# A planner that learns a margin for logit products and GpSimd's hold on VectorE

## The chip, the cores and the metric

The kernel runs on one core of one Trainium2 chip. A core has five engines that run side by side, each with its own queue of instructions: TensorE (PE, matrix products; PEld is its loading of weights), VectorE (DVE), ScalarE (ACT), GpSimd (POOL) and SyncE (SP, which here issues DMAs). They wait for one another by semaphores. The metric is the time of one execution on the device in microseconds (us), the median of several runs.

## The reference

Two stages follow each other. Attention over a window of 128 positions with a distance bias, and then a layer of eight experts in which each token goes to the expert with the highest logit:

```python
scores = scale * np.matmul(q, k.transpose(0, 1, 3, 2))        # 8 batches, 8 heads, 576 x 64
mask = (rel >= 0) & (rel < window)
scores = np.where(mask, scores + bias[None], -1000000000.0)
attn = np.exp(scores - max); attn = attn / (sum + 1e-09)
x = (attn @ v), transposed to 4608 tokens of 512
...
xn = x / (np.linalg.norm(x, axis=-1, keepdims=True) + 1e-06)
logits = xn @ en.T / tau
expert_idx = np.argmax(logits, axis=1)
gate_w = softmax(logits)[expert_idx]
out[mask] = gate_w * (np.maximum(x[mask] @ w1[e], 0.0) @ w2[e])   # w1[e] 512 x 1024, w2[e] 1024 x 512
```

## The kernel before

The 4608 tokens are 36 tiles of 128, numbered T. Two batches make nine tiles: four of each batch and one "pair" tile that holds the last 64 positions of both. The first tile of a batch has no mask to apply. Each tile is worked in two halves of four heads, so there are 72 score units, u = 2T and 2T + 1.

For a unit the steps are: `score` (TensorE, products into two PSUM banks, `sc`), `merge` and `max` (VectorE), `exp` (ScalarE, tile `pe`), `flip` (TensorE transposes into `ptp`), `phi` (ScalarE) and `plo` (VectorE), which read `ptp` and make the two halves of the split probabilities `pq`, `mask` (GpSimd selects, tiles `md` and `mp`, or `tails` for a pair), `av` (TensorE, products with the values), `recip` and `norm` (VectorE, into `xf`). `flip` and `av` share two PSUM banks, so a `flip` also waits until the `plo` of an earlier unit has read its bank.

For a tile there are besides: the loads of q, k and v (SyncE), the turns of q and k (`ptq`, `ptk`; TensorE, into banks that they share with the logits `ptl` and the ranks `ptr`), the split of v (`v_hi`, and `v_lo` on GpSimd, tile `vo`), `xhi` (a cast of `xf` into the row buffer `gx`, mostly on VectorE), `xlo` (GpSimd subtracts the cast from `xf`), `xdma` (a transposing DMA from `gx` to `xT`, issued by SyncE), `logit` (TensorE, L786 and L790) and `lcopy` (VectorE, the copy of the logits that frees their bank). There are 13 row buffers.

The tiles form groups of 8, 8, 8, 6, 4 and 2. A group that is complete goes through some 22 small routing steps, most of them on VectorE with 2 to 64 numbers a partition (L854 to L882: inverse norms, the greatest logit, a one-hot mark, ranks, the gate), with one set of rank products on TensorE between them; then GpSimd marks each row (`mark`, L886) and sends it by an indirect DMA (`put`, L890 and L891, called a scatter here) to the place of its expert in memory.

When the third group is through, the expert with the most tokens so far is known; its weights are fetched and split in the rest of attention, and the first 384 of its rows are worked as the "head" (`hid` and `out`, L971 and L995), which fills TensorE's gaps at the end of attention. Then come the eight experts in turn, with their own plan.

The order on every engine comes from a planner. The class `Plan` holds a list of jobs, each with an engine, a planned length in ns, what it follows (`after`, a name or a name with extra ns), the buffers that it makes and uses, and a due time. It runs through planned time, takes for each engine the ready job that can start first (among those within a small slack the one that is due first), and so writes the instructions of all engines in one order. Real times come into it only through the numbers in the code. The engines keep that order on the chip, and wait where a real time is later than planned. In this code the lines that matter are these:

```python
f"xdma{T}", "SP", 1320, lambda T=T: x_dma(T), land=1000, moves=1350, after=[f"xlo{T}"]
f"logit{T}", "PE", 210 + SWITCH, lambda T=T: logits_pe(T), after=[f"xdma{T}", enc_done]
f"route{gi}_{i}", e, ns + (45 if e == "DVE" else 0), of(gi, 1, i), after=dep
f"wlo{i}", "DVE", 750, lambda i=i: part_lo(i), after=[f"whi{i}"]
```

Of the kernel before, what the change touches and what calls it, by code (L numbers as in the profile page):

```python
# [71 lines left out]
class Plan:  # L72
# [5 lines left out]
    def job(self, name, eng, ns, emit, after=(), makes=(), uses=(), due=0.0, fill=False, early=0.0, dma=0, land=None, moves=0):  # L78
        after = [a if isinstance(a, tuple) else (a, 0) for a in after]
        self.jobs[name] = dict(  # L80
            name=name, eng=eng, ns=ns, emit=emit, after=after, makes=list(makes), uses=list(uses), due=due, fill=fill, early=early, dma=dma, land=land, moves=moves
# [19 lines left out]
    def run(self, free):  # L101
        jobs, rings, end = self.jobs, {}, {}
        self.landed, moved = {}, 0.0
        left = {n: sum(1 for a, _ in j["after"]) for n, j in jobs.items()}
# [7 lines left out]
        def start(j):  # L112
# [5 lines left out]
            for ring, _ in j["makes"]:  # L118
# [3 lines left out]
                if k >= self.caps[ring]:  # L122
                    if k - self.caps[ring] >= len(lst):
                        return None
                    for u in self.users[lst[k - self.caps[ring]]]:
                        if u not in end:
                            return None
                        t = max(t, self.seen(u, j["name"], end))
            return t

        while len(end) < len(jobs):
# [20 lines left out]
            end[n] = t + j["ns"]  # L152
            free[j["eng"]] = end[n]
# [16 lines left out]
def kernel(  # L170
# [238 lines left out]
    def attention(actx):  # L409
# [611 lines left out]
        def due(stage, u):  # L1021
            return STEP * u + 1000 * DUE[stage]
# [25 lines left out]
        for T in range(NT):  # L1048
# [3 lines left out]
            for n in "kq":  # L1052
# [28 lines left out]
                f"v_lo{T}", "POOL", 1070, lambda T=T: v_lo(T), after=[f"v_hi{T}"],  # L1081
                makes=[(vt + "o", ("vo", T))], uses=[("ldv", T), ("vh", T)], due=due("v", u0) + 1500,
            )
            for hf in range(2):
# [10 lines left out]
                for j in range(2):  # L1095
# [28 lines left out]
                    f"mask{u}", "POOL", 0 if first else 1260 if pair else 1188, lambda a=a: mask_pool(*a), after=[f"plo{u}"] + (["tails"] if pair else []),  # L1124
# [21 lines left out]
                f"xhi{T}", "DVE" if dv else "ACT", 400 if dv else 535, lambda T=T: x_act(T),  # L1146
# [3 lines left out]
                f"xlo{T}", "POOL", 1113, lambda T=T: x_pool(T), after=[f"xhi{T}"], uses=[("xf", T), ("gx", T)],  # L1150
# [7 lines left out]
                f"xdma{T}", "SP", 1320, lambda T=T: x_dma(T), land=1000, moves=1350, after=[f"xlo{T}"], makes=[("xT", ("xT", T))], uses=[("gx", T)],  # L1158
# [3 lines left out]
                f"logit{T}", "PE", 210 + SWITCH, lambda T=T: logits_pe(T), after=[f"xdma{T}", enc_done], makes=[(RING["lg"], ("lg", T))],  # L1162
# [18 lines left out]
        for gi, G in enumerate(groups):  # L1181
# [6 lines left out]
            for i, (e, ns) in enumerate(kinds[0]):  # L1188
                dep = [(x, 1500) for x in prev] if i == R_RANK and not tail else list(prev)
                if i == R_RANK and gi:  # L1190
                    dep.append(f"total{gi - 1}")
                J(
                    f"route{gi}_{i}", e, ns + (45 if e == "DVE" else 0), of(gi, 1, i), after=dep, due=due("route", u) + 150 * i,
# [3 lines left out]
                if i == R_RANK - 1:  # L1197
                    J(f"total{gi}", "DVE", 0 if tail else 250, of(gi, 4, 0), after=prev, due=due("route", u) + 5000)
# [501 lines left out]
```

## Time and profile before

| what | us |
|---|---|
| median of 3 runs | 639.07 |
| lowest and highest run | 637.87, 644.59 |
| profiled execution | 639.91 |
| its span, from the first to the last instruction | 638.1 |
| TensorE busy | 604.2 |
| VectorE busy | 383.5 |
| ScalarE busy | 333.7 |
| GpSimd busy | 257.6 |

The profile shows one execution. Its span is what its rows can tell of, and the 1.8 us between the span and the execution's time lie around it. A row's busy time of TensorE counts overlapping products once. "Idle before" is the time an engine stood still before an instruction, and the name behind the arrow is what released it. Names in rows are the program's tiles without their numbers, with the line of the kernel.

### The profile page before, as it was taken

How to read it: one execution, taken by the hardware profiler on the slowest of the kernel's cores; microseconds unless marked ns; L12 is line 12 of the kernel's file. 1: busy time of each engine (PE TensorE's matmuls, PEld its weight loads, DVE VectorE, ACT ScalarE, POOL GpSimd, SP SyncE). 2: the span in 40 equal slices, each digit the busy share in tenths (PEclk: the TensorE clock that was granted, in tenths of full speed). 3: DMA queues.
4: the chain of work that ended last, by engine and by line, in shares of the span. 5: the costliest groups of instructions: out<-in, count | busy, mean ns of one | idle time of the engine just before them, and what ended most of it. 6: DMA issues, size and time to landing. Idle time of an engine off the chain costs nothing. (4 is left out here: it accounts for less than half of the span.)

```text
span 638.1 us, 16989 instructions
## 1 busy us (share of the span) xinstructions
PE 604.2 (95%) x6661; PEld 407.1 (64%) x6661; DVE 383.5 (60%) x1027; ACT 333.7 (52%) x780; POOL 257.6 (40%) x455
## 2 busy tenths in 40 slices
PE   7999889989979878999999999999999999999996
PEld 4788767768767756454664674674765854754444
DVE  4999799898899999707663245334442364310260
ACT  5999789878978985216451144333332263210210
POOL 7878579969878869610102101101102012001001
PEclk9999899989999989999999999999999999999999
DMA  9999979999999967589939129309248073001001
GB/s 190 210 163 190 202 159 220 197 186 219 208 185 281 243 117 191 162 280 216 334 93 328 61 20 282 116 3 301 100 81 317 18 204 119 17 17 50 13 17 50
DMA packets 213585, 101.49 MB, mean 159 GB/s; under 512 B 195829, under 2 KB 195829, under 8 KB 213504
## 3 DMA queue, kind: packets, MB, share of 16 engines
q1 hardware_dynamic: 207664, 81.47, 59.2%
q0 software_dynamic: 5840, 18.92, 7.9%
q8 instruction: 53, 0.87, 0.6%
q14 instruction: 28, 0.23, 0.1%
HBM read 61.92 MB, written 19.70 MB: 128 GB/s over the span
## 5 line engine op out<-in xcount | busy, mean ns | idle before, releaser
L1399 PE MATMUL ps<-xT,w1h 128*128 128x272 f16 (+7 forms) x896 | 173.5, 293 | 0.8 <-ACT y_head L1001 0.8
L1399 PE MATMUL ps<-xT,w1l 128*128 128x272 f16 (+7 forms) x448 | 131.5, 293 | 0.0
L402 POOL DMA_INDIRECT out_dram<-y,ids x32 | 34.1, 1067 | 238.2 <-DVE y L1457 153.0
L1407 DVE SCALAR_TENSOR_TENSOR hl<-ps,hh 128x272 f16<-128x272 f32 (+7 forms) x112 | 52.1, 474 | 95.0 <-ACT hh L1409 94.9
L1399 PEld LDWEIGHTS <-w1h 128*128 128x128 f16 x896 | 87.7, 98 | 31.2 <-issue 1.1
L1409 ACT ACTIVATE hh<-ps 128x272 f16<-128x272 f32 (+7 forms) x112 | 46.6, 426 | 110.9 <-PE ps L1399 110.2
L1443 PE MATMUL ps<-w2h,hl 128*128 128x512 f16 (+1 forms) x264 | 98.4, 373 | 1.3 <-DVE hl L1407 1.3
L1443 PE MATMUL ps<-w2h,hh 128*128 128x512 f16 (+1 forms) x264 | 98.4, 373 | 0.0
L1443 PE MATMUL ps<-w2l,hh 128*128 128x512 f16 (+1 forms) x264 | 98.4, 373 | 0.0
L651 ACT ACTIVATE pe<-sc,nm 128x128 f32<-128x128 f32 x288 | 85.5, 387 | 10.0 <-DVE nm L644 7.3
L1443 PEld LDWEIGHTS <-hh 128*128 128x128 f16 x528 | 51.5, 98 | 58.2 <-issue 0.8
L500 ACT ACTIVATE pq<-ptp 128x512 f16<-128x512 f32 x72 | 55.2, 767 | 9.8 <-PE ptp L659 9.1
L627 PE MATMUL sc<-kh,qh 64*64 64x192 f32 (+3 forms) x1280 | 59.8, 296 | 0.0
L659 PE MATMUL ptp<-ident,pe 128*128 128x128 f32 x288 | 47.0, 284 | 12.6 <-ACT pe L651 4.4
L503 DVE SCALAR_TENSOR_TENSOR pq<-ptp,pq 128x512 f16<-128x512 f32 x72 | 53.1, 737 | 8.3 <-ACT pq L500 8.1
L644 DVE TENSOR_REDUCE nm<-sc 128x2 f32<-128x256 f32 x144 | 55.9, 409 | 0.8 <-PE sc L627 0.8
L1399 PEld LDWEIGHTS <-w1l 128*128 128x128 f16 x448 | 43.8, 98 | 14.5
L1374 DVE SCALAR_TENSOR_TENSOR w1l<-ws,w1h 128x1024 f16<-128x1024 f32 x28 | 33.3, 1221 | 32.0 <-ACT w1h L1376 31.9
L627 PEld LDWEIGHTS sc<-kh,qh 64*64 64x64 f32 (+1 forms) x1280 | 46.0, 143 | 9.2 <-issue 3.9
L727 PE MATMUL av<-vh,mp 128*128 128x65 f16 (+1 forms) x512 | 43.9, 198 | 2.8 <-POOL spare L890 1.8
L1443 PEld LDWEIGHTS <-hl 128*128 128x128 f16 x264 | 25.8, 98 | 31.7 <-DVE hl L1407 2.6
L1455 ACT ACTIVATE y<-ps,gs 128x512 f32<-128x512 f32 (+1 forms) x16 | 10.7, 668 | 67.1 <-PE ps L1443 65.7
(231 smaller groups left out, 1199.9 us busy)
## 6 DMA issues: line engine op xcount, KB each, us to landing
ws<-moe_w_dram SPq DMA_DIRECT2D x56, 512.0 KB, 6.6
ldk<-k_dram SPq DMA_DIRECT2D x32, 256.0 KB, 4.9
ldq<-q_dram SPq DMA_DIRECT2D x32, 256.0 KB, 5.0
ldv<-v_dram SPq DMA_DIRECT2D x32, 256.0 KB
stg<-moe_w_dram SPq DMA_DIRECT2D x16, 256.0 KB, 4.8
ldk<-k_dram SPq DMA_DIRECT2D x8, 128.0 KB, 4.1
ldq<-q_dram SPq DMA_DIRECT2D x8, 128.0 KB, 4.1
ldv<-v_dram SPq DMA_DIRECT2D x8, 128.0 KB, 5.2
```

Source lines behind the costliest of these rows:

```text
L402: ins = nc.gpsimd.indirect_dma_start(out[:, :], bass.IndirectOffsetOnAxis(ap=ids, axis=0), y, None, bounds_check=NTOK - 1, oob_is_err=False)
L500: nc.scalar.activation(hi, ps, AF.Copy, scale=scale)
L503: nc.vector.scalar_tensor_tensor(lo, ps, scale, hi, op0=ALU.mult, op1=ALU.subtract)
L627: nc.tensor.matmul(sc[T, hf, j][o, l, c], qT[T]["h"][rows, hp, o], x["h"][rows, hp, c.start + at : c.stop + at], start=False, stop=True, s ...
L644: nc.vector.tensor_reduce(nm_t[T, hf, j], sc[T, hf, j][:, :, 0:P], axis=AX.X, op=ALU.min)
L651: nc.scalar.activation(pr_t[T, hf][:, 2 * l + j, :], ps[:, l, 0:P], AF.Exp, bias=nm[:, l : l + 1], scale=-1.0)
L659: nc.tensor.transpose(pt[:, i, :], pe[:, i, :], ident)
L727: nc.tensor.matmul(o_, a_, b_, start=False, stop=(n == last), skip_group_check=True)
L1399: nc.tensor.matmul(ps[:, :w], a[:, kt, fs], xx[:, b + kt, c0 : c0 + w], start=(n == 0), stop=(n == len(jobs) - 1))
L1407: nc.vector.scalar_tensor_tensor(hl[:, ft, c0 : c0 + w], ps[:, :w], 0.0, hi, op0=ALU.max, op1=ALU.subtract)
L1409: nc.scalar.activation(hi, ps[:, :w], AF.Relu)
L1443: nc.tensor.matmul(ps, x[:, ft, a * P : (a + 1) * P], w[:, ft, c], start=(n == 0), stop=(n == len(jobs) - 1))
```

## The change

A job may now have a `lock`, a list of lengths for which it holds VectorE off, one after the other from its planned start, and a mark `port`, which says that it is a VectorE step that such a hold stops. A step with `port` that would start within a hold is planned so that it ends 30 ns behind it. The locks go to GpSimd's `v_lo`, `mask` and `xlo`; the mark goes to `xhi` on VectorE, to `wlo`, to `total`, to one gate step and to the routing steps on VectorE except reciprocals, reductions and those that read PSUM. `total` is planned with 300 ns instead of 250 and `wlo` with 650 instead of 750. For all tiles but the last three, `xdma` is planned 800 ns later behind `xlo` and `logit` 1500 ns later behind `xdma`. No instruction is new and none is gone.

```diff
@@ in Plan.run, start(j)
+            if j["port"]:
+                for a, b in held[-8:]:
+                    if a <= t + 60 < b:
+                        t = max(t, b + 30 - j["ns"])
             return t
...
             end[n] = t + j["ns"]
+            if j["port"]:
+                for a, b in held[-8:]:
+                    if a <= t + 60 < b:
+                        end[n] = max(end[n], b + 30)
+            a = t
+            for d in j["lock"]:
+                held.append((a, a + d))
+                a += d
             free[j["eng"]] = end[n]
...
-                f"v_lo{T}", "POOL", 1070, lambda T=T: v_lo(T), after=[f"v_hi{T}"],
+                f"v_lo{T}", "POOL", 1070, lock=(1070,), emit=lambda T=T: v_lo(T), after=[f"v_hi{T}"],
...
-                    f"mask{u}", "POOL", 0 if first else 1260 if pair else 1188, lambda a=a: mask_pool(*a), after=[f"plo{u}"] + (["tails"] if pair else []),
+                    f"mask{u}", "POOL", 0 if first else 1260 if pair else 1188, lock=() if first else (480, 420, 600) if pair else (590, 590), emit=lambda a=a: mask_pool(*a), after=[f"plo{u}"] + (["tails"] if pair else []),
...
-                f"xhi{T}", "DVE" if dv else "ACT", 400 if dv else 535, lambda T=T: x_act(T),
+                f"xhi{T}", "DVE" if dv else "ACT", 400 if dv else 535, port=bool(dv), emit=lambda T=T: x_act(T),
...
-                f"xlo{T}", "POOL", 1113, lambda T=T: x_pool(T), after=[f"xhi{T}"], uses=[("xf", T), ("gx", T)],
+                f"xlo{T}", "POOL", 1113, lock=(1113,), emit=lambda T=T: x_pool(T), after=[f"xhi{T}"], uses=[("xf", T), ("gx", T)],
...
-                f"xdma{T}", "SP", 1320, lambda T=T: x_dma(T), land=1000, moves=1350, after=[f"xlo{T}"], makes=[("xT", ("xT", T))], uses=[("gx", T)],
+                f"xdma{T}", "SP", 1320, lambda T=T: x_dma(T), land=1000, moves=1350, after=[(f"xlo{T}", 800 if T < NT - 3 else 0)], makes=[("xT", ("xT", T))], uses=[("gx", T)],
...
-                f"logit{T}", "PE", 210 + SWITCH, lambda T=T: logits_pe(T), after=[f"xdma{T}", enc_done], makes=[(RING["lg"], ("lg", T))],
+                f"logit{T}", "PE", 210 + SWITCH, lambda T=T: logits_pe(T), after=[(f"xdma{T}", 1500 if T < NT - 3 else 0), enc_done], makes=[(RING["lg"], ("lg", T))],
...
-                    f"route{gi}_{i}", e, ns + (45 if e == "DVE" else 0), of(gi, 1, i), after=dep, due=due("route", u) + 150 * i,
+                    f"route{gi}_{i}", e, ns + (45 if e == "DVE" else 0), port=e == "DVE" and i not in (3, 7, 11, 14, kinds[2] - 1 if gi == GP else 0, kinds[2], kinds[2] + 2), emit=of(gi, 1, i), after=dep, due=due("route", u) + 150 * i,
...
-                    J(f"total{gi}", "DVE", 0 if tail else 250, of(gi, 4, 0), after=prev, due=due("route", u) + 5000)
+                    J(f"total{gi}", "DVE", 0 if tail else 300, port=not tail, emit=of(gi, 4, 0), after=prev, due=due("route", u) + 5000)
...
-                J(f"gate{gi}_{i}", e, ns, of(gi, 2, i), after=prev, due=due("route", u) + 150 * (i + 14))
+                J(f"gate{gi}_{i}", e, ns, port=i == 3, emit=of(gi, 2, i), after=prev, due=due("route", u) + 150 * (i + 14))
...
-            J(f"wlo{i}", "DVE", 750, lambda i=i: part_lo(i), after=[f"whi{i}"], uses=[("stg", i)], due=d + 5500, fill=True)
+            J(f"wlo{i}", "DVE", 650, port=True, emit=lambda i=i: part_lo(i), after=[f"whi{i}"], uses=[("stg", i)], due=d + 5500, fill=True)
```

The order changes on every engine from about the tenth unit to the end of attention; from the experts on it is the same on all of them. Names below are tiles with the tile's and the half's number; the last number is a buffer's. Lines of the changed kernel stand 13 lower than those of before.

VectorE before, where the third group's routing begins (`rc_2`, `rz_2`) and the `plo` of unit 53 writes `pq_26_1`:

```order
L854 TENSOR_SCALAR rc_2_4941<-gn_2_3322 128x8
L743 RECIPROCAL rs_25_1_4943<-av_25_1_4896 128x4
L749 TENSOR_TENSOR xf_25_4849<-av_25_1_4896,rs_25_1_4943 128x256
L765 CAST gx_25_4959<-xf_25_4849 128x512
L857 RECIPROCAL rz_2_4965<-ry_2_4945 128x8
L858 TENSOR_TENSOR rz_2_4965<-rz_2_4965,gn_2_3322 128x8
L859 TENSOR_TENSOR rz_2_4965<-rz_2_4965,ry_2_4945 128x8
L503 SCALAR_TENSOR_TENSOR pq_26_1_4961<-ptp_26_1_4936,pq_26_1_4961 128x512
```

VectorE now, at the same place:

```order
L778 CAST gx_25_4937<-xf_25_4836 128x512
L516 SCALAR_TENSOR_TENSOR pq_26_1_4935<-ptp_26_1_4915,pq_26_1_4935 128x512
L812 COPY gl_2_3617<-ptl_23_4944 128x16
L657 TENSOR_REDUCE nm0_27_1_5001<-sc0_27_1_4925 128x2
L867 TENSOR_SCALAR rc_2_5005<-gn_2_3366 128x8
L657 TENSOR_REDUCE nm1_27_1_5007<-sc1_27_1_4926 128x2
L756 RECIPROCAL rs_26_0_5019<-av_26_0_4953 128x4
L762 TENSOR_TENSOR xf_26_5021<-av_26_0_4953,rs_26_0_5019 128x256
L870 RECIPROCAL rz_2_5032<-ry_2_5014 128x8
L516 SCALAR_TENSOR_TENSOR pq_27_0_5030<-ptp_27_0_5009,pq_27_0_5030 128x512
L871 TENSOR_TENSOR rz_2_5032<-rz_2_5032,gn_2_3366 128x8
```

The `plo` of unit 53 has moved ahead of all routing steps of the group, and the next one ahead of all but two.

TensorE before, at the logit product of tile 16 (`ptl_16`, from `xT_16`), behind the last score product of unit 39 and ahead of the two turns of tile 21; of its eight products and eight weight loads one of each stands here:

```order
L627 MATMUL sc1_19_1_3549<-kh_18_3049,qh_19_3240 64x192
L786 LDWEIGHTS xT_16_3389
L786 MATMUL ptl_16_3576<-enc_169,xT_16_3389 128x16
L511 MATMUL ptk_21_3591<-ident_68,ldk_21_3014 128x128 x4
L511 MATMUL ptq_21_3610<-ident_68,ldq_21_3051 128x128 x4
L659 MATMUL ptp_19_0_3640<-ident_68,pe_19_0_3571 128x128 x4
```

TensorE now, from the same score product on:

```order
L640 MATMUL sc1_19_1_3537<-kh_18_2910,qh_19_3249 64x192
L524 MATMUL ptk_21_3569<-ident_68,ldk_21_2904 128x128 x4
L672 MATMUL ptp_19_0_3579<-ident_68,pe_19_0_3555 128x128 x4
L799 LDWEIGHTS xT_16_3398
L799 MATMUL ptl_16_3588<-enc_169,xT_16_3398 128x16
L724 MATMUL av_18_1_3600<-eone_76,erow_75 128x4
```

The key turn and the flip of unit 38 (`ptp_19_0`) have moved ahead of the logit product.

GpSimd before, from the subtraction ahead of the first scatter on (`xs<-gx` with the tile's number); the memset that stands ahead of every scatter is not shown:

```order
L776 TENSOR_TENSOR gx_10_2310<-xf_10_2212,gx_10_2310 128x512
L891 DMA xs_66<-gx_0_565,di_0_2361 42496x514
L679 AFFINE_SELECT md_11_1_2405<-pq_11_1_2327 128x512
L679 AFFINE_SELECT mp_11_1_2404<-pq_11_1_2327 128x512
L891 DMA xs_66<-gx_1_733,di_0_2361 42496x514
L679 AFFINE_SELECT md_12_0_2469<-pq_12_0_2421 128x512
L679 AFFINE_SELECT mp_12_0_2468<-pq_12_0_2421 128x512
L891 DMA xs_66<-gx_2_879,di_0_2361 42496x514
```

GpSimd now, from the mask of unit 25 (`md_12_1`) to that of unit 28, again without the memsets:

```order
L692 AFFINE_SELECT md_12_1_2541<-pq_12_1_2493 128x512
L692 AFFINE_SELECT mp_12_1_2540<-pq_12_1_2493 128x512
L904 DMA xs_66<-gx_0_565,di_0_2544 42496x514
L904 DMA xs_66<-gx_1_773,di_0_2544 42496x514
L904 DMA xs_66<-gx_2_879,di_0_2544 42496x514
L789 TENSOR_TENSOR gx_11_2495<-xf_11_2353,gx_11_2495 128x512
L904 DMA xs_66<-gx_3_1029,di_0_2544 42496x514
L904 DMA xs_66<-gx_4_1176,di_0_2544 42496x514
L789 TENSOR_TENSOR gx_12_2656<-xf_12_2554,gx_12_2656 128x512
L904 DMA xs_66<-gx_5_1401,di_0_2544 42496x514
L692 AFFINE_SELECT md_14_0_2851<-pq_14_0_2721 128x512
```

The first three scatters stood one by one behind the masks of units 22, 23 and 24, and now stand in a row behind that of unit 25.

## Rows read from the trace of the kernel before

**Rows 1.** The page's first part: busy us, share of the span, instructions.

```profile
PE 604.2 (95%) x6661; PEld 407.1 (64%) x6661; DVE 383.5 (60%) x1027; ACT 333.7 (52%) x780; POOL 257.6 (40%) x455
```

**Rows 2.** Busy us by stretch: length, engines (instructions), granted clock, DMA share, GB/s.

```profile
0.00:36.00 36.00, 31.40 (x444) 23.35 (x445) 26.04 (x84) 28.64 (x76) 29.62 (x83) 1.00 1.10 196
36.00:252.00 216.00, 195.11 (x3737) 157.34 (x3736) 197.28 (x607) 185.22 (x503) 174.68 (x291) 0.98 1.04 197
252.00:279.30 27.30, 25.69 (x156) 12.94 (x154) 15.99 (x72) 7.42 (x17) 14.14 (x31) 1.00 0.61 181
279.30:638.10 358.80, 352.01 (x2328) 213.45 (x2327) 144.20 (x266) 112.38 (x185) 39.13 (x52) 1.00 0.42 131
...
36.00:80.00 44.00, 41.95 (x825) 34.58 (x824) 36.77 (x112) 39.74 (x109) 31.16 (x46) 0.96 1.14 188
80.00:96.00 16.00, 13.28 (x239) 10.70 (x236) 14.90 (x51) 13.19 (x37) 12.30 (x28) 1.00 0.73 156
96.00:129.40 33.40, 32.80 (x660) 26.53 (x659) 30.09 (x87) 30.13 (x85) 30.61 (x46) 1.00 1.11 201
129.40:142.00 12.60, 10.04 (x183) 8.30 (x183) 12.56 (x46) 9.45 (x25) 8.13 (x23) 0.86 1.15 206
142.00:182.00 40.00, 37.89 (x750) 30.78 (x742) 36.18 (x104) 36.94 (x105) 36.56 (x57) 1.00 1.09 207
182.00:198.00 16.00, 12.80 (x275) 10.43 (x276) 15.71 (x59) 11.90 (x32) 11.38 (x26) 1.00 1.23 217
198.00:216.00 18.00, 17.11 (x309) 13.93 (x306) 16.08 (x46) 16.20 (x44) 17.10 (x27) 1.00 1.16 278
216.00:237.00 21.00, 16.49 (x341) 13.19 (x337) 20.67 (x67) 19.14 (x52) 13.82 (x26) 0.92 0.86 166
237.00:252.00 15.00, 12.75 (x197) 8.90 (x190) 14.33 (x43) 8.53 (x22) 13.63 (x20) 1.00 0.59 156
```

**Rows 3.** TensorE's waits, 36 to 262 us: total us, times, longest.

```profile
PE ptl L786 <- DMA xT<-gx: 3.5, 4, 1.7
...
PE av L727 <- POOL tails L692: 1.4, 2, 1.0
```

**Rows 4.** TensorE's timeline at four waits: start, us, what, [idle before <-releaser].

```profile
66.82 0.26 PE L786 MATMUL ptl<-enc,xT 128*128 128x16 f16 x4 [1.74 <-DMA xT<-gx]
...
130.15 0.26 PE L786 MATMUL ptl<-enc,xT 128*128 128x16 f16 x4 [0.68 <-DMA xT<-gx]
...
132.17 0.33 PE L511 MATMUL ptq<-ident,ldq 128*128 128x128 f32 x1 [1.17 <-DVE gl L799]
...
182.71 0.55 PE L659 MATMUL ptp<-ident,pe 128*128 128x128 f32 x3 [1.62 <-DVE rz L860]
```

**Rows 5.** VectorE's timeline ahead of the flip at 182.71.

```profile
180.69 1.12 DVE L858 TENSOR_TENSOR rz<-rz,gn 128x8 f32<-128x8 f32 x1
181.85 0.17 DVE L859 TENSOR_TENSOR rz<-rz,ry 128x8 f32<-128x8 f32 x1
```

**Rows 6.** GpSimd's timeline over the same time.

```profile
180.64 1.15 POOL L776 TENSOR_TENSOR gx<-xf,gx 128x512 f16<-128x512 f32 x1
```

**Rows 7.** GpSimd's scatters by line: ns min/median/max, first and last start.

```profile
L891 POOL DMA_INDIRECT xs<-gx,di x36: 963/982/1559, 88.3 to 268.6; - x36
```

**Rows 8.** Timeline where the experts begin, SyncE and TensorE.

```profile
272.13 2.18 SPq L1305 DMA_TRANSPOSE xT<-xs  x1
...
279.34 0.40 PE L1399 MATMUL ps<-xT,w1h 128*128 128x288 f16 x2 [0.78 <-ACT y_head L1001]
```

**Rows 9.** The columns of rows 2, for three stretches of low clock.

```profile
68.00:71.40 3.40, 3.40 (x51) 2.39 (x48) 1.08 (x4) 2.54 (x8) 1.41 (x5) 0.50 1.04 184
132.90:136.30 3.40, 3.25 (x52) 2.93 (x56) 3.37 (x14) 3.05 (x8) 1.83 (x9) 0.51 1.30 239
231.90:235.30 3.40, 3.08 (x52) 2.27 (x44) 3.08 (x17) 3.17 (x9) 1.35 (x8) 0.51 0.24 44
```

**Rows 10.** TensorE's timeline, the products of one score unit without its bias.

```profile
96.88 0.82 PE L627 MATMUL sc<-kh,qh 64*64 64x192 f32 x16
```

More of the change, by code (lines that the diff above doesn't have):

```diff
@@ L76, in __init__, with job @@
         self.jobs, self.caps, self.users = {}, {}, {}
-    def job(self, name, eng, ns, emit, after=(), makes=(), uses=(), due=0.0, fill=False, early=0.0, dma=0, land=None, moves=0):
+    def job(self, name, eng, ns, emit, after=(), makes=(), uses=(), due=0.0, fill=False, early=0.0, dma=0, land=None, moves=0, port=False, lock=()):
         after = [a if isinstance(a, tuple) else (a, 0) for a in after]
         self.jobs[name] = dict(
-            name=name, eng=eng, ns=ns, emit=emit, after=after, makes=list(makes), uses=list(uses), due=due, fill=fill, early=early, dma=dma, land=land, moves=moves
+            name=name, eng=eng, ns=ns, emit=emit, after=after, makes=list(makes), uses=list(uses), due=due, fill=fill, early=early, dma=dma, land=land, moves=moves, port=port, lock=lock
         )
@@ L103, in run @@
         self.landed, moved = {}, 0.0
+        held = []
         left = {n: sum(1 for a, _ in j["after"]) for n, j in jobs.items()}
```

## The prediction

> **What bounds the kernel now.** I read the busy shares first, then the same shares cut into stretches, then the waits of TensorE, and last the instructions around the longest of them. TensorE is busy 95% of the span [rows 1], so only its idle time and the time it spends at a low clock can be won. The stretches [rows 2] say where that is: from 279.3 us on (the experts) it idles 6.8 us of 358.8, and the change leaves every engine's order there as it is; the first 36 us idle 4.6, and TensorE's order is the same for nearly all of them; the head's products from 252 to 279.3 idle 1.6. What is at stake is 36 to 252 us, where 216 us hold 195.1 of work: 20.9 idle. The reader should see two kinds of stretch there. In four (80 to 96, 129.4 to 142, 182 to 198, 216 to 237) TensorE works 52.6 of 65.6 us (20% idle) while VectorE is busy 63.8 (97%); in the other five TensorE works 142.5 of 150.4 (5% idle) with VectorE at 89%. The four are where the small routing steps of a group of tiles stand on VectorE, between the steps that TensorE waits for. The waits proper are few and long: logit products for their transposing DMA, 3.5 us in four [rows 3], the first 1.74 and another 0.68, and right behind the latter a turn that waits 1.17 for the copy of those logits, since they share a bank [rows 4]; a flip that waits 1.62 at 182.7 [rows 4] for a `plo` behind routing steps, one of which took 1.12 us where its like took 0.17 [rows 5], while GpSimd ran a subtraction over the same time [rows 6]; and two value products behind the pair masks, 1.4 us [rows 3].
>
> **The change part by part.** No instruction is added or removed; the planner's other numbers make another order up to the experts, on all engines.
>
> (a) Logit margin. A logit product is now placed 1.5 us later behind its DMA, and the DMA 0.8 us later behind GpSimd's subtraction, but for the last three tiles. At tile 16 the order sets a key turn and a flip ahead of the logit product, so I count the 0.68 and the 1.17 behind it as gone. At tile 6 one key turn and one value product more stand ahead, others fewer; I take half, 0.9 of the 1.74. The remaining two of the four waits sum to 1.1; one of them is tile 35's, which the margin leaves out, so 0.5. Sum 3.3; a DMA that is queued later can be late for another logit, for which I take 0.5 off: 2.8. Bounds: 0 and 4.7 (all four and the turn). What hangs on the later logits is the routing chain and the scatters, not a product of attention, until the 13 row buffers are full; the buffer's scatter keeps its place ahead of the step that needs it in GpSimd's order.
>
> (b) Routing steps spread. In the order of before, the third group has four routing steps ahead of the `plo` that frees the flip's bank at 182.7; in the new one that `plo` stands ahead of all of them. The steps of the first, second and fourth group now spread over five or six score units instead of three or four. If the four stretches idled at the quiet rate (5% of 65.6 = 3.5 us) TensorE would win 13.0 - 3.5 = 9.5, less the 1.85 that (a) has counted: 7.6. It can't be all, because VectorE's work doesn't shrink but for the holds: 197.3 us in 216 is 91% now, and in 206 would be 96%. I take two thirds, 5.0; bounds 0 (the lag only moves) and 7.6.
>
> (c) The end of attention. GpSimd's order now sets the last two pair masks ahead of all scatters of the fourth group's tiles; before, two and one stood among them. Six small marks take the scatters' place ahead of the first. Of the 1.4 us [rows 3] I take half, 0.7 (bounds 0 and 1.4). The price is three more scatters behind the last mask, at 0.98 [rows 7] and a memset each, some 3.8 us. Their cover is GpSimd's own idle time there (14.1 busy of 27.3 [rows 2]). What is late next would be the rows of the first expert: their DMA is issued at 272.13, while TensorE starts on them at 279.34 when the head's last result has left its bank [rows 8]. So TensorE's work after attention sets that start, not the scatters.
>
> (d) The clock. Three times the granted clock fell to half (0.50 or 0.51 in the rows, the lower of its two levels) for 3.4 us, with TensorE busy 3.40, 3.25 and 3.08 of it [rows 9]: 9.7 us of work that takes 4.9 at the full clock. Each followed a stretch with long waits (the 1.74; the 0.68 and 1.17; one just ahead of 231.9 us); some of the other long waits cost no clock. Counting half of the three as avoided gives 2.4; bounds 0 and 4.9.
>
> (e) What the new order costs. In GpSimd's order the scatters of the first group stood one by one among the masks; now three stand in a row behind the mask of unit 25 and three more before the next real mask, and four behind that of unit 41: 3.8 us more ahead of a mask. TensorE's order answers by setting a score product more (0.82 us [rows 10] and its bias), a flip and a value product ahead, some 2.2 us by estimate, for the first burst and two of each for the second. That leaves 1.6 uncovered, and new waits of the same making elsewhere: flips of some units stand closer to their scores than before (unit 45 above all), which I bound by as much again. I take +3.0; bounds 0 and 10.
>
> The hold has another direction, which the change doesn't plan. The row: GpSimd's 36 scatters take 0.96 at the least, the middle one 0.98 and the longest 1.56 [rows 7]. If all of that is VectorE's hold, it is 0.6 us at most and nothing for the common case, so the sum has nothing for it and a rival below has the 0.6. The Trainium skill (SBUF — State Buffer, "SBUF: two separate sides") says the port pair is an exclusive lock that works both ways, the loser blocking fully, and that a DMA whose descriptors GpSimd writes is starved behind a two-port VectorE step (some 620 ns alone, 3100 beside a copy). By that page's price the seven scatters in bursts could each take 2.5 us more, an estimate of 17 us on GpSimd, and the change would come out slower; the longest scatter here, 1.56, doesn't bear that out.
>
> Sum: -2.8 - 5.0 - 0.7 - 2.4 + 3.0 = -7.9 us. The profiled execution took 639.91 (span 638.1), 0.8 above the median of 639.07, so I set the sum against the median: **631 us**.
>
> **The rivals.**
> *More than that.* VectorE keeps up once the routing steps are spread and fewer are held: (a) 3.8, (b) 7.6, (c) 0.7, (d) 3.5, against 1.6 of new waits: -14, so 625. For it: VectorE is at 89% in the quiet stretches. Against: ScalarE and VectorE would both have to run near full.
> *The waits only move.* VectorE has the same steps, the lag spreads over more units and TensorE pays it in small pieces; the clock falls as often elsewhere. Only (a) is left, less 1 us: 637.3. For it: VectorE at 97% in the four stretches is bound by work, of which the holds are a part only. The planner would then not do what it is told to: its locks stand at planned times, and GpSimd's real times drift from them.
> *Slower.* The bursts decide. GpSimd is busy 30.6 of 33.4 us from 96 to 129.4 [rows 2], so a backlog of 3.8 us stays there. From the point where a mask lands over 1.6 us after TensorE has come to its value product, each of the two bursts costs 1.6 and a fall of the clock 1.6 more [rows 9], 6.4 in all; the norm, the transposing DMA and so the logit behind it come late as well, which gives (a) back, and nothing of (b) is left. Where VectorE holds the seven scatters by 0.6 each [rows 7], half of those 4.2 us meet TensorE too: +8.5, so 647.5. Against: TensorE's order has moved the value products back by 2 us or more just there.
>
> **How the numbers follow.** Forecast (627.5 to 635) 0.52, more 0.17, the waits only move 0.21, slower 0.10. A measurement of this kernel can tell about 1% from no change, that is 632.7 below and 645.5 above. Three quarters of the forecast's case and all of the stronger one lie below 632.7: 0.39 + 0.17 = 0.56 faster. Same is the rest of the forecast and the case in which the waits move: 0.13 + 0.21 = 0.34; slower 0.10. The range leaves out the tenth that is slower and about as much of the strong case: 624 to 640.
>
> **What would show it.** In the profile after: (a) TensorE waits for the transposing DMA under 1.5 us in all from 36 us to the end of attention, and no turn behind a logit copy; (b) no flip that waits over 1 us with a routing step as its releaser, the four groups of small steps drawn out over five units, and a mean of `rz` products with `gn` clearly under the present longest of 1.12; (c) the head ending near 270 and the experts starting with it, their part as long as before (358.8 us); (d) one or two falls of the clock before 250 us instead of three; (e) value products of units 28 and 42 that wait no more than 1 us for a mask. It would be wrong if the value products wait for masks or scatters by several us, if the rows of the first expert land after the head's end, or if VectorE shows no less held time and TensorE's idle time up to 252 us is still near 20.

## The result and the profile after

The median went from 638.92 us (16 runs) to 634.57 us (16 runs), 4.35 us less. The ratio on record, which isn't that of the two medians (0.9932), is 0.9919 with an interval of 0.9898 to 0.994, or 5.2 us less (3.8 to 6.5). The side and the range of the prediction hold; the size is between half and two thirds of the 7.9 us in its sum. The profiled executions, 639.91 and 632.89 us, differ by 7.0, more than the medians do, so their rows show somewhat more gain than a typical run has.

The page's first part and the busy times by stretch of the changed kernel, with the columns of [rows 1] and [rows 2]; the third line ends where the experts begin:

```profile
PE 601.7 (95%) x6661; PEld 403.5 (64%) x6661; DVE 378.0 (60%) x1027; ACT 331.8 (53%) x780; POOL 257.4 (41%) x455
```

```profile
0.00:36.00 36.00, 32.36 (x451) 24.15 (x452) 25.75 (x84) 29.54 (x79) 30.26 (x85) 1.00 1.11 189
36.00:252.00 216.00, 200.00 (x3802) 158.19 (x3801) 199.67 (x631) 185.89 (x508) 178.44 (x300) 1.00 1.09 205
252.00:271.10 19.10, 17.13 (x86) 7.77 (x85) 8.54 (x48) 3.99 (x9) 9.33 (x19) 1.00 0.56 177
271.10:630.80 359.70, 352.23 (x2328) 213.38 (x2327) 144.03 (x266) 112.38 (x185) 39.36 (x52) 1.00 0.43 131
...
80.00:96.00 16.00, 15.31 (x260) 12.13 (x260) 15.40 (x54) 14.59 (x41) 13.61 (x29) 1.00 0.84 191
...
129.40:142.00 12.60, 11.60 (x218) 9.38 (x217) 12.57 (x45) 11.15 (x31) 10.85 (x23) 1.00 1.10 189
...
182.00:198.00 16.00, 13.70 (x267) 11.01 (x259) 15.97 (x62) 12.55 (x35) 11.99 (x26) 1.00 1.15 217
...
216.00:237.00 21.00, 18.30 (x361) 13.89 (x362) 20.97 (x77) 18.91 (x53) 16.64 (x30) 1.00 0.93 143
```

Read these against [rows 2]. The experts begin at 271.1 instead of 279.3, 8.2 us earlier, and then take 359.7 instead of 358.8. Ahead of that point TensorE was busy 31.4 + 195.1 + 25.7 = 252.2 of 279.3 before and is busy 32.4 + 200.0 + 17.1 = 249.5 of 271.1 now. So idle time fell from 27.1 to 21.6 (5.5 us) and busy time by 2.7, with the same products: the granted clock reads 1.00 in every stretch, where 36 to 252 us had 0.98. VectorE's whole busy time fell by 5.5 us (383.5 to 378.0) with the same instructions. A second profile of the changed kernel (e6_after_again) shows less of each: the experts begin at 273.8 us, 5.5 us earlier than before, with 23.6 us idle and 250.2 busy ahead of them, and VectorE's busy time is 380.9, 2.6 less than before.

TensorE's waits of the changed kernel from 36 to 262 us (total us, times, longest), and then the flips' largest in the kernel before, with a wait for GpSimd that [rows 3] leaves out:

```profile
PE ptp L672 <- DVE pq L516: 4.1, 7, 1.1
PE ptp L672 <- DVE rs L756: 2.7, 4, 0.9
PE ptp L672 <- ACT pe L664: 2.4, 5, 1.0
PE ptp L672 <- ACT w1h L952: 1.3, 1, 1.3
PE ptr L845 <- DVE oh L882: 1.2, 1, 1.2
PE av L724 <- DVE pq L516: 1.0, 1, 1.0
PE ptl L799 <- DMA xT<-gx: 0.9, 3, 0.4
PE av L740 <- POOL mp L692: 0.6, 2, 0.4
...
PE ptp L672 <- ACT ry L869: 0.3, 1, 0.3
```

```profile
PE ptp L659 <- ACT pe L651: 4.2, 5, 1.4
PE ptp L659 <- DVE rn L862: 2.0, 1, 2.0
PE av L727 <- POOL spare L890: 1.8, 6, 0.6
PE ptp L659 <- DVE rz L860: 1.6, 1, 1.6
PE ptp L659 <- DVE pq L503: 1.6, 4, 0.8
...
PE ptp L659 <- DVE rs L743: 1.0, 1, 1.0
```

The logit products wait 0.9 us for their DMA instead of 3.5 [rows 3], no turn waits behind a logit copy, and the waits behind the tails (1.4 in [rows 3]) are gone. Before, the value products also waited 1.8 us behind the small memsets ahead of the scatters (`spare`) and 0.7 behind masks; now they wait 0.6 for GpSimd in all. The flips are another matter. Summed over all releasers, the small ones left out here too, they waited 11.4 us and wait 11.3. What released them changed: routing steps (`rn`, `rz`, `lg`, `oh`, and now `ry`) from 4.1 to 0.8, `plo` and the reciprocal (`pq`, `rs`) from 2.6 to 6.8.

The other side of that is on VectorE. The routing products of the line whose longest took 1.12 us [rows 5], and the casts of the routed rows, each over the whole span (min/median/max ns), first after, then before:

```profile
L871 DVE TENSOR_TENSOR rz<-rz,gn x6: 144/150/259, 75.0 to 253.7; 128x8 f32<-128x8 f32 x3, 128x6 f32<-128x6 f32 x1, 128x4 f32<-128x4 f32 x1, 128x2 f32<-128x2 f32 x1
...
L778 DVE CAST gx<-xf x34: 404/484/1806, 21.4 to 242.8; 128x512 f16<-128x512 f32 x34
```

```profile
L858 DVE TENSOR_TENSOR rz<-rz,gn x6: 152/494/1122, 76.6 to 262.2; 128x8 f32<-128x8 f32 x3, 128x6 f32<-128x6 f32 x1, 128x4 f32<-128x4 f32 x1, 128x2 f32<-128x2 f32 x1
...
L765 DVE CAST gx<-xf x34: 409/444/1414, 21.6 to 252.5; 128x512 f16<-128x512 f32 x34
```

In this profile no routing product of this line takes over 0.26 us; the casts are held longer. From 20 to 250 us a cast took 645 ns in the mean (34 of them) against 545 before (33), some 3.4 us more in all. The worst one shows how. GpSimd, VectorE and TensorE of the changed kernel around 158 us (start, us, what, [idle before <-releaser]):

```profile
157.50 0.65 POOL L692 TENSOR_SCALAR_AFFINE_SELECT md<-pq 128x512 f32<-128x512 f32 x1
158.08 0.64 POOL L692 TENSOR_SCALAR_AFFINE_SELECT mp<-pq 128x512 f32<-128x512 f32 x1
...
158.72 0.63 POOL L692 TENSOR_SCALAR_AFFINE_SELECT md<-pq 128x512 f32<-128x512 f32 x1
159.30 0.82 POOL L692 TENSOR_SCALAR_AFFINE_SELECT mp<-pq 128x512 f32<-128x512 f32 x1
```

```profile
157.83 1.81 DVE L778 CAST gx<-xf 128x512 f16<-128x512 f32 x1
...
159.89 0.71 DVE L516 SCALAR_TENSOR_TENSOR pq<-ptp,pq 128x512 f16<-128x512 f32 x1
```

```profile
160.66 0.18 PE L724 MATMUL av<-eone,erow 128*128 128x4 bf16 x1 [1.04 <-DVE pq L516]
```

The cast starts inside one mask step, three more follow with hardly a pause, and it ends inside the fourth, 0.3 us after the third has ended (159.35 us) and 1.4 us later than its minimum of 0.40 would have it. The `plo` behind it is late, and TensorE's value product waits 1.04 us for that.

The end of the head, on SyncE and TensorE of the changed kernel:

```profile
264.06 2.32 SPq L1318 DMA_TRANSPOSE xT<-xs  x1
```

```profile
257.06 0.18 PE L845 MATMUL ptr<-oh,tri 128*128 128x16 bf16 x1 [1.20 <-DVE oh L882]
...
271.11 0.41 PE L1412 MATMUL ps<-xT,w1h 128*128 128x288 f16 x2 [0.78 <-ACT y_head L1014]
```

As in [rows 8], the first expert's rows are asked for 7.1 us ahead of its first product, and what releases that product is the head's last result: the head sets the start. A longer wait stands ahead of it: the last rank product stands 1.2 us for `oh`, 0.25 in the profile before.

### The profile page after: what moved, and what is told of

It is laid out like the page before. It is cut to its first block, busy times and chain, and to the rows that moved or that the text cites. A ratio compares the mean times of both kernels' runs of the same rounds, so it can differ in the third digit from the quotient of the medians.

```text
span 630.8 us, 17006 instructions
## 1 busy us (share of the span) xinstructions
PE 601.7 (95%) x6661; PEld 403.5 (64%) x6661; DVE 378.0 (60%) x1027; ACT 331.8 (53%) x780; POOL 257.4 (41%) x455
## 5 line engine op out<-in xcount | busy, mean ns | idle before, releaser
L640 PE MATMUL sc<-kh,qh 64*64 64x192 f32 (+3 forms) x1280 | 58.2, 289 | 0.0
L1387 DVE SCALAR_TENSOR_TENSOR w2l<-ws,w2h 128x1024 f16<-128x1024 f32 x28 | 33.9, 1222 | 20.7 <-ACT w2h L1389 20.7
L1389 ACT ACTIVATE w1h<-ws 128x1024 f16<-128x1024 f32 x28 | 28.4, 1052 | 33.5 <-DMA ws<-moe_w_dram 33.5
```

Source lines behind the costliest of these rows:

```text
L640: nc.tensor.matmul(sc[T, hf, j][o, l, c], qT[T]["h"][rows, hp, o], x["h"][rows, hp, c.start + at : c.stop + at], start=False, stop=True, s ...
L1387: nc.vector.scalar_tensor_tensor(lo_, x, SW, hi, op0=ALU.mult, op1=ALU.subtract)
```

## The experiments

Each ratio is to the kernel before on the same chip. The kernel before took 643.54, 638.54 and 639.03 us in the median in the three rounds, so times of different rounds don't compare in us, and their profiles do only stretch by stretch. Two theories stood against each other at first: A, that the gain is the margin's (logit waits and the low clock that follows them); B, that it is the knowledge of the hold (routing steps no longer held, the order around them). The first four runs take them apart.

**e1_margin**: the kernel before with the two margins alone.

```diff
-            f"xdma{T}", ..., after=[f"xlo{T}"], ...
+            f"xdma{T}", ..., after=[(f"xlo{T}", 800 if T < NT - 3 else 0)], ...
-            f"logit{T}", ..., after=[f"xdma{T}", enc_done], ...
+            f"logit{T}", ..., after=[(f"xdma{T}", 1500 if T < NT - 3 else 0), enc_done], ...
```

> Before plus the two margins alone. Theory A (the gain is the logit margin's: waits for the transposing DMA from 3.5 us to about 1, the turn behind a logit copy gone, and with them falls of the clock): 3 to 5 us faster than before, so 634 to 636, and TensorE's waits for the DMA under 1.5 us. Theory B (the gain is the planner's knowledge of the hold): within 1.5 us of before. Theory C (any new order moves the time this much): no telling from this run alone.

Measured: 1.0005, interval 0.9982 to 1.0028. Its waits of TensorE:

```profile
PE ptp L659 <- ACT pe L651: 5.1, 9, 2.1
PE ptp L659 <- DVE pq L503: 4.8, 7, 1.4
PE ptp L659 <- DVE lg L864: 1.8, 1, 1.8
PE ptp L659 <- DVE lg L863: 1.4, 1, 1.4
...
PE ptl L786 <- DMA xT<-gx: 1.1, 2, 0.6
```

The margin does what it says to the logits (3.5 us to 1.1), the profile has one fall of the clock instead of three, and nothing is won: flips behind `pe`, `pq` and `lg` alone now wait 13.1 us, where those of the kernel before wait 11.4 behind all releasers. Theory A, as a cause by itself, falls.

**e2_port**: the change without the margins (locks, marks and the two lengths).

```diff
-            f"xdma{T}", ..., after=[(f"xlo{T}", 800 if T < NT - 3 else 0)], ...
+            f"xdma{T}", ..., after=[f"xlo{T}"], ...
-            f"logit{T}", ..., after=[(f"xdma{T}", 1500 if T < NT - 3 else 0), enc_done], ...
+            f"logit{T}", ..., after=[f"xdma{T}", enc_done], ...
```

> Before plus locks and marks alone (with the two changed lengths), no margin. Theory A: within 2 us of before, TensorE still waits 3 us or more for the transposing DMA. Theory B: 3 to 5 us faster than before, the held time of the routing steps down by more than half. If both parts count and add up, this and the run with the margins alone sum to about -4.4 us.

Measured: 0.9945, interval 0.992 to 0.9971, some 3.5 us less than before. The reader should see that it gains although the logits wait three times as long as before:

```profile
PE ptl L799 <- DMA xT<-gx: 11.4, 13, 2.1
```

The execution that was profiled took 642.36 us, 2.4 above the median of the kernel's fast runs, so its rows can't show where the gain lies. In these two runs most of the result comes with the hold's part. What the margins add to it (0.9945 to 0.9919) is less than the two intervals can tell apart, though the waits they aim at go from 11.4 to 0.9 us.

**e3_lengths**: the kernel before with the two planned lengths alone, as a control for how much any small edit of the planner's numbers does.

```diff
-  J(f"total{gi}", "DVE", 0 if tail else 250, ...
+  J(f"total{gi}", "DVE", 0 if tail else 300, ...
-  J(f"wlo{i}", "DVE", 750, ...
+  J(f"wlo{i}", "DVE", 650, ...
```

> Before with the two changed lengths alone (300 for the total, 650 for the low weight parts): no margin, no lock. It is a control: nothing in it bears on a wait. Theories A and B: within 1.5 us of before. Theory C (a new order by itself moves the time by about half a per cent): 2 us or more off, to either side.

Measured: 1.0006, interval 0.9982 to 1.0029; three falls of the clock, as before.

**e5_vector_load**: the changed kernel with one more reciprocal in each of the 72 units, into a tile that nobody reads, in place between the others.

```diff
+    nc.vector.reciprocal(sm.tile([P, 4], F32, tag="rx", ...), xps[T, hf][:, :, D])
```

> The changed kernel with one more reciprocal of the same 128 x 4 numbers for each of the 72 units, which nobody reads; the planner doesn't know of it and the order is the same. It adds 72 steps, by the row of the like step 0.17 us each, with overlap 0.1: 7 to 12 us of VectorE work in attention. If VectorE bounds attention (the waits only move): 6 to 10 us slower than the changed kernel. If TensorE does and VectorE's lateness is a matter of single steps: 1 to 3 us slower.

Measured: 0.9991, interval 0.9972 to 1.0009. Against the change's 0.9919 that is 0.7%, some 4.6 us (2.8 to 6.4, an estimate from the two intervals). The added steps, and one of them with the step behind it:

```profile
L757 DVE RECIPROCAL rx<-av x72: 138/149/168, 15.4 to 252.8; 128x4 f32<-128x4 f32 x72
...
106.49 0.15 DVE L757 RECIPROCAL rx<-av 128x4 f32<-128x4 f32 x1
106.56 0.39 DVE L657 TENSOR_REDUCE nm<-sc 128x2 f32<-128x256 f32 x1
```

The durations sum to 72 x 0.15 = 10.8 us, but rows of neighbouring steps overlap: the next step starts 0.07 us behind the start of the added one (the middle of the 72; 5.6 us in all). So a microsecond taken from VectorE's queue costs about 0.8 us of the time (0.5 to 1.1, an estimate): that is nearer to the case in which VectorE bounds attention than to the other. Part of it may be the clock's, which is low from 150.8 to 157.8 us in this profile and nowhere in the change's. VectorE's busy time is no measure of this price. It is 379.0 us here, against 378.0 and 380.9 in the two profiles of the change, though 72 steps were added: the casts, for one, sum to 20.4 us against 21.9 and 23.9.

The next four runs ask which part of the change matters, and whether a longer planned hold makes the casts better.

**e6_after_again**: the changed kernel itself, for a second profile.

> The changed kernel unaltered, beside the other three on the same chip. All theories: 0.992 of before (0.990 to 0.994). If it comes out near the locks and marks alone (0.9945), the margin adds nothing to them; if at 0.992 or below, it adds some 1 to 2 us though it gave nothing by itself. A second profile of it also shows what of the first one's waits is chance: theory A expects TensorE's waits for the DMA near 1 us again and its waits at flips near 12.

Measured: 0.9922, interval 0.9894 to 0.9951; the logits wait 0.5 us for their DMA, the flips behind `pq`, `rs` and `pe` 5.8, 2.8 and 2.4 us and in all 12.7, the last rank product 1.4; the longest cast takes 2.13 us; no fall of the clock in attention. In these points the first profile showed the order's doing and not one execution's. In one point the second differs. A routing product and the wait of a flip behind it:

```profile
74.80 1.06 DVE L871 TENSOR_TENSOR rz<-rz,gn 128x8 f32<-128x8 f32 x1
...
PE ptp L672 <- DVE rz L872: 1.2, 1, 1.2
```

GpSimd's subtraction runs from 74.68 to 75.84 us there. So the same order held this step in one execution and not in the other: the planner's locks stand at planned times, and the real ones drift.

**e7_logit_margin**: the change without the 0.8 us ahead of the transposing DMA.

```diff
-            f"xdma{T}", ..., after=[(f"xlo{T}", 800 if T < NT - 3 else 0)], ...
+            f"xdma{T}", ..., after=[f"xlo{T}"], ...
```

> The changed kernel without the 0.8 us on the DMA, with the 1.5 us on the logit product. If the margin works by giving the DMA time to land, this is all of it: the waits for the DMA stay near 1 us and the time is that of the changed kernel within 1.5 us. If the place in SyncE's queue counts, 2 us or more slower.

Measured: 0.9956, interval 0.9934 to 0.9977; the waits for the DMA are 0.9 us here too. In this order the logits' margin of 1.5 us clears them. It is 0.34 to 0.37% slower than the change; whether the 0.8 adds that is inside the intervals.

**e8_no_cast_mark**: the change without the mark that tells the planner that VectorE's cast is held.

```diff
-            f"xhi{T}", "DVE" if dv else "ACT", 400 if dv else 535, port=bool(dv), emit=...
+            f"xhi{T}", "DVE" if dv else "ACT", 400 if dv else 535, emit=...
```

> The changed kernel with the mark on the routing steps, the total, the gate step and the low weight parts, not on the cast into the row buffer. In the changed kernel the casts were held by 7.4 us in all against 3.7 before, the routing steps by about 1.5 against 6.5. If the mark on the cast does nothing (the cast is chained to GpSimd's steps anyway), the time stays within 1.5 us and the casts' held time near 7; if the mark keeps them from worse, 2 to 4 us slower with over 9 us held.

Measured: 1.0014, interval 0.9993 to 1.0035. All of the gain is gone, yet its casts are held less than the change's (569 ns in the mean from 20 to 250 us against 645). New long waits stand in its place:

```profile
PE ptp L672 <- DVE pq L516: 3.9, 4, 1.8
...
PE av L724 <- DVE xf L762: 2.9, 5, 1.6
...
PE ptp L672 <- DVE rz L872: 1.2, 1, 1.2
```

So held time on the casts isn't what the result turns on; another order came out, and it is a worse one. The marks on the routing steps, the largest term of the sum, are all in this kernel. They don't bring the gain by themselves, and they don't keep the steps free: a product of the line of [rows 5] takes 1.07 us in it.

**e9_longer_holds**: the change with the planner starting a marked step as if each hold lasted 120 ns longer.

```diff
-                    if a <= t + 60 < b:
-                        t = max(t, b + 30 - j["ns"])
+                    if a <= t + 60 < b + 150:
+                        t = max(t, b + 150 - j["ns"])
```

> The changed kernel with each hold planned 120 ns longer for the choice of a start (a marked step goes 150 ns behind a hold's end, not 30). If what is left of the holds is the drift between planned and real times on GpSimd, the held time falls from 10.8 us in all to under 8 and the kernel is 1 to 3 us faster; if VectorE is bound by its work, or the order is as good as it gets, within 1.5 us or slower.

Measured: 0.9986, interval 0.9961 to 1.0011, with a mean granted clock of 0.984 in its profile and four falls of it up to the head's end (two of them in a row). The casts take 610 ns in the mean, not much less than the change's 645. A more careful planner is not a faster kernel here.

The last four runs weigh the clock, and ask how much of the result belongs to the one order that the change's numbers draw.

**e10_filler**: the kernel before, its order kept, with products that nobody reads ahead of the logits of tiles 6, 16 and 31, to fill the waits ahead of the three low clocks of [rows 9].

```diff
-            lg = bank("lg", [P, 512], name=f"ptl_{T}")[:, 0 : 2 * E]
+            lg = bank("lg", [P, 512], name=f"ptl_{T}")
+            for _ in range({6: 8, 16: 6, 31: 8}.get(T, 0)):
+                nc.tensor.matmul(lg, ones, brow..., start=True, stop=True, ...)
+            lg = lg[:, 0 : 2 * E]
```

> The kernel before, in its order, with products that nobody reads put on TensorE ahead of three logit products, into the logits' own bank, 8 at tile 6, 6 at tile 16 and 8 at tile 31 (512 columns each, some 0.22 us): they fill the long waits after which the clock fell at 68.0, 132.8 and 231.8 us. If half the gain of the change is the clock's (theory D), the falls go and the kernel is 2 to 4 us faster than before though it does 4.8 us more work on TensorE; if the falls are a by-product that costs nothing, it is 0 to 3 us slower.

Measured: 1.0009, interval 0.9993 to 1.0025. The three low clocks are gone (two others came, at 15.5 and 182.7 us), and over its 12 executions the mean granted clock is 0.997, where the kernel before has 0.993 on that chip. The same three stretches as in [rows 9]:

```profile
68.00:71.40 3.40, 3.40 (x74) 2.74 (x71) 2.14 (x6) 2.73 (x8) 1.89 (x3) 1.00 0.66 149
132.90:136.30 3.40, 2.78 (x66) 2.29 (x64) 3.37 (x15) 2.95 (x8) 1.31 (x9) 1.00 1.07 185
231.90:235.30 3.40, 2.25 (x54) 1.65 (x52) 3.37 (x19) 3.30 (x9) 1.50 (x9) 1.00 0.40 76
```

In the first TensorE is the busy engine, and 74 products run where 51 did. TensorE's timeline on either side of it, the logit product of tile 6 and the first product of a score unit, in this kernel, and then the latter in the one before, whose logit product stands in [rows 4] at 66.82:

```profile
67.77 0.25 PE L789 MATMUL ptl<-enc,xT 128*128 128x16 f16 x4
...
71.98 0.41 PE L608 MATMUL sc<-brow,bcol 64*64 64x512 bf16 x4
```

```profile
72.55 0.41 PE L608 MATMUL sc<-brow,bcol 64*64 64x512 bf16 x4
```

From 0.95 us behind to 0.57 ahead: this one was worth 1.5 us. In the other two VectorE is busy 3.37 of 3.40 us and TensorE's busy time falls from 3.25 to 2.78 and from 3.08 to 2.25: at the full clock it stands idle instead. By the first products of score units on either side the second was worth nothing (0.50 us behind at 128.9, 0.51 at 141.8) and the third 0.4 (0.31 behind at 231.9, 0.07 ahead at 236.2). So here a fall of the clock cost 1.5 us where TensorE set the pace and 0.4 or less where VectorE did. That the sum comes to no gain isn't wholly told by this: two falls came elsewhere, and a logit product that didn't wait before stands 1.38 us for its DMA at 116.15 us.

**e11_margins_less** and **e13_margins_more**: the change with margins of 1.3 and 0.7 us, and of 1.7 and 0.9 us.

```diff
-  ... (f"xlo{T}", 800 if ...)    ... (f"xdma{T}", 1500 if ...)
+  ... (f"xlo{T}", 700 if ...)    ... (f"xdma{T}", 1300 if ...)      # e11_margins_less
+  ... (f"xlo{T}", 900 if ...)    ... (f"xdma{T}", 1700 if ...)      # e13_margins_more
```

> The changed kernel with 1.3 and 0.7 us for the margins instead of 1.5 and 0.8, which gives another order. If what the planner knows makes the gain, 0.990 to 0.995 of before; if the order of the change is a lucky draw (theory C), anywhere between 0.992 and 1.002, with falls of the clock where it is slow.

> The changed kernel with 1.7 and 0.9 us for the margins. Knowledge: 0.990 to 0.995 of before, waits for the transposing DMA still near 1 us. Luck: anywhere between 0.992 and 1.002.

Measured: 0.9994, interval 0.9969 to 1.0019, for the smaller margins, without a fall of the clock in attention; 0.9921, interval 0.9896 to 0.9946, for the larger, with two falls (201.9 and 229.2 us). With the larger margins one logit product still waits 2.3 us for its DMA, against the 1 us that was expected. The kernel whose profile has no falls gains nothing and the one with two is as fast as the change: the count of falls in a profile doesn't order the times.

**e12_locks_more**: the change with each planned lock of GpSimd's long steps 10 or 20 ns longer.

```diff
-  v_lo: lock=(1070,)    mask: (590, 590)    xlo: lock=(1113,)
+  v_lo: lock=(1090,)    mask: (600, 600)    xlo: lock=(1133,)
```

> The changed kernel with the holds planned 10 to 20 ns longer (1090, 1133, 600 and 600 instead of 1070, 1113, 590 and 590), another order again. Knowledge: 0.990 to 0.995 of before. Luck: anywhere between 0.992 and 1.002.

Measured: 0.9967, interval 0.9937 to 0.9996; the logits wait again, with the margins in place, and the clock doesn't fall:

```profile
PE ptl L799 <- DMA xT<-gx: 4.8, 6, 1.9
```

All orders beside each other:

| order | ratio | falls of the clock in its profile, up to the head's end | mean granted clock of its executions |
|---|---|---|---|
| before | 1 | 3 | 0.992 to 0.994 |
| e1_margin | 1.0005 | 1 | 0.992 |
| e3_lengths | 1.0006 | 3 | 0.993 |
| the change | 0.9919, 0.9922 | 0 | 0.997, 0.998 |
| e13_margins_more | 0.9921 | 2 | 0.994 |
| e2_port | 0.9945 | 2 | 0.996 |
| e7_logit_margin | 0.9956 | 0 | 0.998 |
| e12_locks_more | 0.9967 | 0 | 0.996 |
| e9_longer_holds | 0.9986 | 4 | 0.990 |
| e11_margins_less | 0.9994 | 0 | 0.996 |
| e8_no_cast_mark | 1.0014 | 1 | 0.996 |

A profile is one execution; the last column has them all, and it doesn't order the times either. Within one kernel a lower clock can go with a longer time: e12_locks_more took 632.5 to 634.1 us at a clock of 0.999 and 635.8 to 640.9 at 0.994 or less. Whether that is the price of the falls or of the waits ahead of them isn't shown.

The eight orders that were planned with the hold have a mean of 0.9963 (give or take 0.003, an estimate from their spread), about 2.4 us less than before, and spread over 0.95%, about 6 us, though some of them differ by 0.2 us in a margin, 10 or 20 ns in a lock, or one mark alone. The three planned without it lie within 0.06%. That the knowledge helps on the average is what this suggests; that the change is one of the better draws, this shows.

## Why the prediction held in side and range, and not in size

**(a) The logit margin**, forecast at -2.8. The waits went about as sized: 3.5 + 1.17 for the turn before, 0.9 after, 3.8 less. The step that an avoided wait is an equal gain of time fails by itself: e1_margin takes 2.4 us of the same waits away and wins nothing, while its flips wait longer. Only beside the hold's part can some of it have counted, and that isn't resolved (e2_port against the change).

**(b) The routing steps**, forecast at -5.0: this is the term that was mis-sized. Its mechanism is there in the first profile. The longest `rz` product of the line of [rows 5] went from 1.12 to 0.26 us (1.06 in the second profile), flips released by routing steps from 4.1 to 0.8, and the four stretches (of time; the work in them has moved) idle 16 + 12.6 + 16 + 21 - (15.31 + 11.60 + 13.70 + 18.30) = 6.7 us instead of 13.0. But the flips of the whole stretch wait as long as before (11.3 and 11.4), now behind `plo` and the reciprocal, the other five stretches idle 9.3 instead of 7.9, and the casts carry 3.4 us of hold more. I had argued that VectorE's work sets a limit and still took two thirds of the bound; counted on the flips themselves next to nothing of it came. The rival "the waits only move" described this term, and e5_vector_load bears its reason out: time taken from VectorE's queue costs 0.8 us per us, and the change leaves VectorE's work as it is but for the holds. Yet of the two parts run alone it is the one with the locks that gains (0.9945), and the marks on the routing steps without the one on the cast gain nothing (1.0014). Waits and single runs so put the gain in different places, and neither shows the part that makes it.

**(c) The end of attention**, forecast at -0.7. The two waits behind the tails went (1.4), and that of the last rank product grew from 0.25 to 1.2 and 1.4. The experts start when the head ends, at 271.1, and their part is as long as before within 0.9 us.

The hold's other direction stayed where [rows 7] had it. The scatters of the changed kernel:

```profile
L904 POOL DMA_INDIRECT xs<-gx,di x36: 956/977/1459, 91.3 to 260.5; - x36
```

The Trainium skill (SBUF — State Buffer, "SBUF: two separate sides") has descriptors of GpSimd starved behind two-port steps of VectorE; this trace doesn't show that for the scatters in their new places, the longest of which takes 1.46 us, while the middle one lands 5.6 us after its issue instead of 5.2.

**(d) The clock**, forecast at -2.4 for half of three falls. All three went in both profiles, and the busy time ahead of the experts fell by 2.7 and 2.0 us. But e10_filler removes the same three and gains nothing: two of them lay where TensorE waited for VectorE, and the busy time saved came back as idle time. The count was too careful and the price too high: 4.9 us for the three, where e10_filler shows 1.9 beside them.

**(e) The new order's cost**, forecast at +3.0. The bursts of scatters cost nothing where I put them: no value product of units 28 and 42 waits for a mask in the first profile (in the second one of unit 28 stands 0.9 us, without a releaser in the profile), so the rival "slower" had no ground. This term had the wrong sign where it was looked for: all waits of value products for GpSimd fell from 3.9 us (`spare` 1.8, the tails 1.4 of (c), `mp` 0.7) to 0.6. The cost showed at the casts and the flips instead.

The five terms of the sum are waits taken one by one. What came is a start of the experts 8.2 us earlier in the one profiled execution, made of 5.5 us less idle and 2.7 us less busy time, 5.5 us earlier in the other, and 4.35 us in the medians. That the sum came out on the right side owes something to luck: two terms that fell short, (b) and (d), stand beside one that was taken for a cost and was none, and neighbouring settings of the same idea gave anything from 0.9921 to 1.0014.

What stays open: which property makes one planned order better than another. Logit waits (11.4 us in e2_port, 0.9 in e7_logit_margin, with ratios of 0.9945 and 0.9956), the hold on the casts (less in e8_no_cast_mark, with no gain) and the clock each fail to order the times.

## What to carry to other kernels

Where a planner sets the order, teaching it holds across engines promises more than margins do (0.9945 against 1.0005 alone), but judge such a change by several neighbouring settings: here 0.2 us in a margin, or one mark, moved the time as much as the whole change did. A wait that is taken away is worth its length only if the next engine isn't nearly full: measure that engine's price first, by adding a known load to it (here 0.8 us per us), and count the load from the start of a step to the start of the next, since the durations of neighbouring rows overlap. A low clock is to be priced by the engine that sets the pace in its stretch, not by the work that runs slower.

## What the runs showed of the hardware that was not expected

A VectorE step that is held isn't always let go between GpSimd steps that follow each other closely: the cast at 157.83 us stayed through three mask steps and took 1.81 us, 2.13 in the second profile at its worst, for a minimum of 0.40. Others got through behind the first: the cast at 101.24 us took 0.73, with one mask step to 101.68 and the next from 101.62 to 102.46. So the price of starting a held step inside a chain can be that of several GpSimd steps; what decides it isn't shown.

A VectorE step of 128 x 4 numbers has a row of 0.15 us and delays the step behind it by 0.07 (e5_vector_load).

Three falls of the granted clock to its lower level, 3.4 us each, could be removed from the kernel before without any change in its time (e10_filler, 1.0009), with two falls elsewhere in its profile and a mean clock of 0.997 instead of 0.993 over all executions.
